# A dual attention kernel with a token gate: gate logits gathered in one bank with one transpose, the gate's load moved, and a new order of the whole

## The chip, the cores and the metric

The kernel runs on one core of one Trainium2 chip, in one launch. The metric is the device time in microseconds; the median of three runs stands for the kernel.

## The reference

One input x of 2048 tokens by 512 features passes through two branches, and a gate mixes them token by token. All arrays are bf16.

```python
g = sigmoid((x * gate_w).sum(-1, keepdims=True))
# A: softmax attention, H = 32 heads of Dh = 16
scores = einsum("bhqd,bhkd->bhqk", q, k) * Dh ** -0.5
a = einsum("bhqk,bhkd->bhqd", softmax(scores), v) ... @ A_wo
# B: linear attention with a learned feature map
phi(y) = concat([softmax(y @ w_phi), softmax(-y @ w_phi)])
kv = einsum("bhsf,bhsd->bhfd", phi(k), v);  z = phi(k) summed over s
b = (phi(q) @ kv) / (phi(q) @ z + 1e-6) ... @ B_wo
return g * a + (1 - g) * b
```

q, k and v of each branch come from x @ A_wqkv and x @ B_wqkv. Branch A needs 32 x 2048 x 2048 exponentials, and these are nearly all of the work.

## The kernel before

**Units and packs.** The scores of branch A are cut into units of 128 keys by 512 queries for one head. Four heads make a pack (four units, stacked in the four row groups of TensorE), 16 packs (all 2048 keys) make a head group, and 32 such groups (8 for each of the four token quarters) make 512 packs and 2048 units. `_scores` (L981) computes scores into PSUM. `_exp` (L1031) runs the exponential on ScalarE over three and two units in turn, through a ring of five PSUM banks, into the tile ET. `_values` (L1101) multiplies ET with V and sums the pack into one bank for the head group; V carries a column of ones, so the softmax sum comes with it. `_norm` transposes this sum in 32x32 blocks on VectorE (L1161), divides and transposes back.

**Units on VectorE.** Some units skip ScalarE. `SHARES` lists how many for each of the 32 head groups. `_plan_vector` (L835) places them, always as the fourth unit of a pack, and collects them in batches of `NB` = 5; `FIRST` and `LAST` give the sizes of the first and last batches, `SOON` four single packs near the start that are handled in two early batches. `_vector_batch` (L866) computes the scores of each unit into a bank, turns them into fixed-point bits on VectorE (L887, one instruction a unit), and then a cubic approximation of the exponential for the whole batch (L911, L913, L914, L915, L897) into the tile vu.

**Branch B and projections.** VectorE also copies out the projections (L703, L759, L783), does branch B's feature maps (L1272 and L1300 to L1354) and the normalizations. `K0`, `SK`, `Q0`, `SQ` are due times of branch B's parts, counted in packs.

**The order.** Every operation is registered with an engine, an assumed cost, a priority `prio` and a release `rel` (in packs). `Plan.order` simulates the engines and writes out a fixed order for each engine's queue; the waits on semaphores follow from the data. So at run time each engine works through a fixed list, and TensorE and SP stop at the first instruction whose input is missing. Assumed DMA sizes (`size`, in MB) only tell the simulation when data will land. `rel` is not a wait on the chip: it only decides the place in the list. Three PSUM banks outside the ring are handed to jobs (accumulators, projections, gate, VectorE's units) in that order.

**Loads.** `_loads` (L497) registers all loads on SP but one. Those of WA (A_wqkv) come in two parts, the first 128 columns of each of q, k, v at the start and the other 384 columns later, with `rel` = `XREL`. WB is B_wqkv, WoA and WoB are the output weights, and gw is the gate vector, in 2-byte pieces to 128 partitions. Two token quarters of x are transposed by DMA (L604), and so are two parts of WB (L1231).

**The gate.** `_gate` (L788) spreads the gate vector over 128 columns on POOL (gwb, L791). For each token quarter four matmuls (L800) give the quarter's logits, the same in all 128 rows of a bank of its own. VectorE transposes that bank in 32x32 blocks into T1 (L805) and copies one column out into gz (L808). Then come sign, one exponential (L816), plus one, and a copy to four partition groups (L822).

Of the kernel before, what the change touches and what calls it, by code (L numbers as in the profile page):

```python
# [7 lines left out]
ALU = mybir.AluOpType  # L8
AX = mybir.AxisListType

P = 128
# [6 lines left out]
F32, BF16 = dt.float32, dt.bfloat16  # L18
# [349 lines left out]
class _Kernel:  # L368
# [2 lines left out]
    NSLOT = 25  # L371
    VCP = 8 * 17 + 16
    NQS = 6
    NB, NVU, LEAD = 5, 3, 11
    QDUE, VPRIO, VREL, TPRIO = 27.0, -9.0, 161.0, 3
    KEEP = 14
    XREL, KD, VD = 12, 11, 5
    BYDMA = (2, 3)
    KREL = 2
    EARLY = 23  # L380
    VREL0 = 3
    FIRST = (2, 2)
    LAST = (3, 2)
    OREL = 0

    def __init__(self, nc, A_x, A_wqkv, A_wo, B_wqkv, B_w_phi, B_wo, gate_w, out):
        self.nc = nc
# [27 lines left out]
    def _memory(self, ctx):  # L415
        nc, S, NT, NQC = self.nc, self.S, self.NT, self.NQC
# [80 lines left out]
    def _loads(self):  # L497
        NT = self.NT
        B = Buf
        self.b_xn = [[B(), B()] for _ in range(self.NQC)]  # L500
        self.b_WA = [[B(), B()] for _ in range(3)]
        self.b_WB = [B(), B(), B()]
        self.b_WoA, self.b_WoB, self.b_wphi, self.b_gw = B(), B(), B(), B()
        self.b_wphin, self.b_heads = B(), B()
        WA3 = self.A_wqkv.rearrange("(c p) j -> p c j", p=P)
        x4 = self.x2d.rearrange("(t p) d -> p t d", p=P)

        WB3 = self.B_wqkv.rearrange("(c p) j -> p c j", p=P)

        def load_x(j, t0, n, prio, rel=-99):  # L510
            writes = self.b_xn[j] if n == 4 else [self.b_xn[j][t0 % 4 // 2]]
            self.dma("SP", f"x{j}{t0 % 4 // 2}", lambda e: e.dma_start(self.xn[:, t0:t0 + n, :], x4[:, t0:t0 + n, :]),
                     writes=writes, prio=prio, cost=0.53, rel=rel, size=0.131 * n)

        def load_wa(s, part, eng, prio, rel=-99):
            lo, hi = (0, P) if part == 0 else (P, D)
            self.dma(eng, f"wa{s}{part}", lambda e: e.dma_start(
                self.WA[:, s, :, lo:hi], WA3[:, :, D * s + lo:D * s + hi]), writes=[self.b_WA[s][part]], prio=prio,
                cost=0.54, rel=rel, size=0.131 if part == 0 else 0.393)

        def load_wb(s, prio, rel=-99):
            self.dma("SP", f"wb{s}", lambda e: e.dma_start(self.WB[:, s], WB3[:, :, D * s:D * s + D]),
                     writes=[self.b_WB[s]], prio=prio, rel=rel, cost=0.53, size=0.524)
# [16 lines left out]
        self.dma("SP", "gw", lambda e: e.dma_start(self.gw[:], self.gate_w.rearrange("(c p) -> p c", p=P),  # L540
                                                   allow_slow_non_contiguous=True),
                 writes=[self.b_gw], prio=-4, cost=0.53, rel=6, size=0.016)
# [244 lines left out]

    def _gate(self):  # L788
        op, NQC = self.plan.op, self.NQC
        b_gwb, last = Buf(), []  # L790
        op("POOL", lambda e: e.tensor_copy(self.gwb[:], self.gw[:, :, None].to_broadcast([P, 4, P])), 1.0,  # L791
           reads=[self.b_gw], writes=[b_gwb], name="gwb", prio=15)
        z = self.gz[:]
        for qc in range(NQC):
            job = Job()

            m = None
            for c in range(4):
                def mm(e, c=c, qc=qc, job=job):
                    return e.matmul(self._bank(job), self.gwb[:, c, :], self.xT[:, 4 * qc:4 * qc + 4, c],  # L800
                                    start=(c == 0), stop=(c == 3))
                m = op("PE", mm, self.c_pe(512), reads=[self.b_xT[qc], b_gwb], deps=[m], name="gate", prio=18 + qc,
                       rel=12, acquire=None if c else job)
            k = qc % 2
            t = op("DVE", lambda e, k=k, job=job: e.transpose(  # L805
                self.T1[:, k].rearrange("p b d -> p (b d)"), self._bank(job)), 0.65, deps=[m], name="gate_t",
                prio=18 + qc, writes=[self.b_T1[k]], release=job)
            last.append(op("DVE", lambda e, qc=qc, k=k: e.tensor_copy(self.gz[:, qc], self.T1[:, k, :, 0]), 0.2,  # L808
                           reads=[self.b_T1[k]], name="gate_c", prio=18 + qc))
        flat = self.gh[:].rearrange("p r q b -> p (r q b)")  # L810
        col = z.rearrange("p q b -> p (q b)")
        for r, sign in ((0, -1.0), (1, 1.0)):
            last.append(op("DVE", lambda e, r=r, sign=sign: e.tensor_scalar(
                self.gh[:, r].rearrange("p q b -> p (q b)"), col, sign, None, op0=ALU.mult), 0.2,
                deps=list(last), name="gate_z", prio=22))
        a = op("ACT", lambda e: e.activation(flat, flat, ACT.Exp), 0.2, deps=last, name="gate_exp", prio=24)  # L816
        self.b_g, self.b_hB = Buf(), Buf()
# [1 line left out]
               name="gate_h", prio=24)  # L819
        parts = []  # L820
        for j in range(4):
# [13 lines left out]
    def _plan_vector(self):  # L835
# [746 lines left out]
```

## Time and profile before

| | |
|---|---|
| median of 3 runs | 840.32 us (840.21 to 841.15) |
| the profiled execution, its own time | 842.38 us |
| its span, first to last instruction | 838.9 us |
| busy: TensorE / VectorE / ScalarE / POOL | 803.5 / 809.9 / 826.7 / 8.1 us |
| granted TensorE clock | 1.000 |

The engines are written PE (TensorE), PEld (its weight loads), DVE (VectorE), ACT (ScalarE), POOL (GpSimd) and SP. Times in the profile are of one profiled execution, which lies 3.48 us over its span and 2.06 us over the median of the runs. A group's line gives busy time, the mean of one instruction in ns, the idle time of the engine just before, and what ended most of that idle time. In a timeline, the first two columns are the start and the length in us, and a bracket at the end holds the engine's wait just before it. Instructions of one engine overlap a little, so the distance from one start to the next is the better cost of one.

### The profile page before, as it was taken

The page shows a single profiled execution, that of the slowest core. Times are in us where ns is not written, and L with a number is a line of the kernel's source. Part 1 is how long each engine was busy: PE and PEld are TensorE (multiplying, and loading weights), DVE is VectorE, ACT ScalarE, POOL GpSimd, SP SyncE. Part 2 cuts the span into 40 slices and gives each one's busy share as a digit, 9 for nine tenths or more (in the row PEclk, how much of TensorE's full clock was granted, in tenths as well). Part 3 has the DMA queues.
Part 4 walks back from the last instruction along what each step waited for, and adds up shares of the span by engine and source line. Part 5 has one row for each costly group of instructions (what it writes and reads, how often), then busy time and mean ns, then how long its engine had stood idle before and what let it go on. Part 6 is the DMA issues. An engine that isn't in the chain of part 4 may idle for free.

```text
span 838.9 us, 19684 instructions
## 1 busy us (share of the span) xinstructions
PE 803.5 (96%) x8800; PEld 265.3 (32%) x8800; DVE 809.9 (97%) x1055; ACT 826.7 (99%) x733; POOL 8.1 (1%) x14
## 2 busy tenths in 40 slices
PE   9999999999999999999999999999999999999998
PEld 4334233233322322232223222332223332222344
DVE  5999999999999999999999989999999999999996
ACT  7999999999999999999999999999999999999997
POOL 3000000000000000000000000000000000000000
PEclk9999999999999999999999999999999999999999
DMA  9600000000000000030003000320002110000000
GB/s 227 183 1 3 5 2 7 1 2 8 2 7 2 8 1 8 2 65 19 1 15 81 14 8 2 57 52 1 8 2 52 33 32 2 2 7 2 2 2 27
DMA packets 49027, 20.01 MB, mean 24 GB/s; under 512 B 38704, under 2 KB 48944, under 8 KB 48944
## 3 DMA queue, kind: packets, MB, share of 16 engines
q1 hardware_dynamic: 48272, 18.58, 9.9%
q8 instruction: 68, 1.11, 0.6%
q10 hardware_dynamic: 672, 0.20, 0.1%
q14 instruction: 15, 0.12, 0.1%
HBM read 6.31 MB, written 2.10 MB: 10 GB/s over the span
## 4 chain that ended last, share of the span: by engine, by line
ACT 75%; DVE 16%; PE 4%; DMA 2%; SPq 2%; issue 0%
ACT ET L1039 75%; DVE vt L887 2%; DVE vu L897 2%; PE ps L988 2%; DVE vf L914 1%; DMA WA<-in_A_wqkv_dram 1%; PE ps L1117 1%; DVE vu L915 1%; DVE bq L1272 1%; DVE vf L911 1%; DMA WB<-in_B_wqkv_dram 1%; DVE vt L1315 1%; PE ps L1108 1%; SPq L604 1%; DVE bq L1309 1%; DVE V L783 1%
## 5 line engine op out<-in xcount | busy, mean ns | idle before, releaser
L1039 ACT ACTIVATE ET<-ps 128x1536 bf16<-128x1536 f32 x728 | 824.4, 1381 | 2.8 <-PE ps L988 2.3
L988 PE MATMUL ps<-qT,kT 32*128 32x512 bf16 (+2 forms) x2248 | 318.3, 364 | 26.8 <-ACT ET L1039 20.6
L1117 PE MATMUL ps<-kT,zero 128*32 128x512 bf16 (+1 forms) x3100 | 259.9, 383 | 0.0
L1108 PE MATMUL ps<-ET,V 128*32 128x512 bf16 (+2 forms) x1993 | 196.3, 364 | 0.7 <-DVE vt L887 0.4
L988 PEld LDWEIGHTS ps<-qT,kT 32*128 32x128 bf16 x2248 | 84.0, 91 | 305.0 <-ACT ET L1039 217.6
L887 DVE TENSOR_SCALAR vt<-ps 128x512 uint32<-128x512 f32 x224 | 145.1, 678 | 4.5 <-PE ps L988 4.0
L897 DVE SCALAR_TENSOR_TENSOR vu<-vt,vu 128x2560 int16<-128x2560 uint32 (+2 forms) x47 | 126.4, 2690 | 0.5
L1117 PEld LDWEIGHTS ps<-kT,zero 128*32 128x32 bf16 x3100 | 70.2, 94 | 109.0 <-issue 82.5
L1108 PE MATMUL ps<-vu,V 128*32 128x512 bf16 (+1 forms) x255 | 84.1, 360 | 0.0
L1108 PEld LDWEIGHTS ps<-ET,V 128*32 128x32 bf16 x1993 | 56.1, 95 | 58.4 <-issue 31.0
L915 DVE TENSOR_TENSOR vu<-vu,vf 128x2560 f16<-128x2560 f16 (+2 forms) x49 | 67.8, 1385 | 0.5
L914 DVE TENSOR_TENSOR vf<-vf 128x2560 f16<-128x2560 f16 (+2 forms) x49 | 67.8, 1385 | 0.2
L911 DVE TENSOR_SCALAR vf<-vt 128x2560 f16<-128x2560 uint8 (+2 forms) x47 | 66.7, 1418 | 0.0
L681 PE MATMUL ps<-WB,xT 128*128 128x512 bf16 x192 | 55.4, 383 | 1.1 <-DVE T L1161 1.0
L913 DVE TENSOR_SCALAR vu<-vf 128x2560 f16<-128x2560 f16 (+2 forms) x49 | 37.6, 767 | 0.2
L681 PE MATMUL ps<-xT,WA 128*128 128x512 bf16 (+1 forms) x124 | 35.3, 379 | 1.5 <-DMA WA<-in_A_wqkv_dram 1.3
L1108 PEld LDWEIGHTS ps<-vu,V 128*32 128x32 bf16 x255 | 22.4, 96 | 13.0 <-issue 8.4
L1161 DVE STREAM_TRANSPOSE T<-ps 128x512 f32<-128x512 f32 (+1 forms) x35 | 23.1, 660 | 2.1 <-PE ps L1108 2.0
L681 PEld LDWEIGHTS ps<-WB,xT 128*128 128x128 bf16 x192 | 14.2, 97 | 26.7 <-issue 14.4
L1272 DVE TENSOR_SCALAR bq<-ps 128x512 bf16<-128x512 f32 x32 | 21.3, 679 | 0.6 <-PE ps L681 0.5
L777 PE MATMUL ps<-WA,xT 128*128 128x128 bf16 x256 | 19.3, 220 | 0.0
L1315 DVE TENSOR_TENSOR vt<-vt,brec 128x4096 bf16<-128x4096 bf16 (+1 forms) x10 | 18.6, 1864 | 0.3
(100 smaller groups left out, 432.3 us busy)
## 6 DMA issues: line engine op xcount, KB each, us to landing
qT<-qraw SPq DMA_DIRECT2D x120, 16.0 KB, 1.8
xn<-in_A_x_dram SPq DMA_DIRECT2D x3, 512.0 KB, 6.8
WB<-in_B_wqkv_dram SPq DMA_DIRECT2D x3, 512.0 KB, 6.1
out_dram<-WB SPq DMA_DIRECT2D x12, 128.0 KB, 1.7
WA<-in_A_wqkv_dram SPq DMA_DIRECT2D x3, 384.0 KB, 8.7
xn<-in_A_x_dram SPq DMA_DIRECT2D x2, 256.0 KB, 3.8
WoA<-in_A_wo_dram SPq DMA_DIRECT2D x1, 512.0 KB, 8.3
WoB<-in_B_wo_dram SPq DMA_DIRECT2D x1, 512.0 KB, 9.0
```

The lines of the kernel that those rows point to most:

```text
L681: mm = op("PE", lambda e, c=c: e.matmul(self._bank(job)[:, 0:n], lhs(c), rhs(c), start=(c == 0), stop=(c == 3)), self.c_pe(n), reads=reads ...
L887: parts.append(op("DVE", lambda e, j=j, job=job: e.tensor_scalar(vt[:, j, :], self._bank(job), SCALE * LOG2E * 2.0 ** 24, 2.0 ** 31, op0=A ...
L897: o = op("DVE", lambda e: e.scalar_tensor_tensor(out=flat(vu).bitcast(I16), in0=flat(vt), scalar=2.0 ** -17, in1=flat(vu), op0=ALU.mult, o ...
L911: ("_frac", two, lambda e: e.tensor_scalar(vf, frac, 1 / 256, ROOT, op0=ALU.mult, op1=ALU.add), [b_vt], [b_vf]),
L913: lambda e: e.tensor_scalar(vu, vf, CUBE, SQUARE, op0=ALU.mult, op1=ALU.add), [b_vf], [b_vu]),
L914: ("_sq", two, lambda e: e.tensor_tensor(vf, vf, vf, ALU.mult), [b_vf], [b_vf]),
L915: ("_cube", two, lambda e: e.tensor_tensor(vu, vu, vf, ALU.mult), [b_vf, b_vu], [b_vu]),
L988: ins = e.matmul(out[u][:, cols], self.kT[32 * i:32 * i + 32, cp, kt * TOK:(kt + 1) * TOK], self.qT[32 * i:32 * i + 32, s, q], start=True, ...
L1039: o = plan.op("ACT", lambda e: e.activation(self.ET[:, a % NS:a % NS + n, :], self.ps[:, a % NR:a % NR + n, :], ACT.Exp, scale=SCALE), sel ...
L1108: ins = e.matmul(self._bank(ot)[32 * i:32 * i + 32, to], self.V[:, kt, g8 // 2, v0:v0 + 32], tile[:, cols], start=first and j == 0, stop=o ...
L1117: ins = e.matmul(self._bank(ot)[32 * i:32 * i + 32, lo:QCH], self.zero[:], self.kT[:, 0, lo:QCH], start=False, stop=False, tile_position=( ...
L1272: [lambda e, b, k=k: e.tensor_scalar(bq[:, k].rearrange("p (g s v) -> p g s v", g=8, s=2)[:, :, 0, :], b.rearrange("p (g v) -> p g v", g=8 ...
```

## The change

The gate's four quarters share one bank. The buffer gwb is 136 columns wide, is set to zero, and gets the gate vector in columns 6, 38, 70 and 102. Reading 128 columns from column 6 - 2 qc puts the vector at column 2 qc of each group of 32, so quarter qc's logits land in rows 2 qc of every 32 rows and zeros are added to the others. All sixteen matmuls add into one bank, one transpose brings the logits out, and the sign is applied straight from T1, so the copies into gz are gone. The first gate matmul now needs all four quarters of x. The gate vector's load gets a later place (`rel` 12, priority -0.3, behind WoA at -1 and WoB at -0.5) and a larger assumed size. The rest are constants of the order: `XREL` 12 to 6 for the later parts of WA, a larger assumed size for them, other releases, priorities and due times, and other SHARES. With `ENDS` = 11 in place of 9 and eight units in place of nine in the last head group, the last of them lies in pack 510 of 0 to 511; before, none lay in the last four packs.

```diff
-    NB, NVU, LEAD = 5, 3, 11
-    QDUE, VPRIO, VREL, TPRIO = 27.0, -9.0, 161.0, 3
+    NB, NVU, LEAD = 5, 3, 26
+    QDUE, VPRIO, VREL, TPRIO = 27.0, -12.0, 161.0, 4
-    XREL, KD, VD = 12, 11, 5
+    XREL, KD, VD = 6, 11, 4
-    KREL = 2
-    EARLY = 23
-    VREL0 = 3
+    KREL = 3
+    EARLY = 19
+    VREL0 = 5
-    LAST = (3, 2)
-    OREL = 0
+    LAST = (4,)
+    OREL = 2
+    ENDS = 11
...
-        self.gwb = sb("gwb", [P, 4, P], BF16)
+        self.gwb = sb("gwb", [P, 4, P + 8], BF16)
-        self.gz = sb("gz", [P, NQC, 16], F32)
...
-                cost=0.54, rel=rel, size=0.131 if part == 0 else 0.393)
+                cost=0.54, rel=rel, size=0.131 if part == 0 else 0.45)
...
-                 writes=[self.b_gw], prio=-4, cost=0.53, rel=6, size=0.016)
+                 writes=[self.b_gw], prio=-0.3, cost=0.53, rel=12, size=0.1)
...
+        op("POOL", lambda e: e.memset(self.gwb[:], 0.0), 0.6, writes=[b_gwb], name="gwb_zero", prio=-10)
+        op("POOL", lambda e: e.tensor_copy(
+            self.gwb[:, :, 6:134].rearrange("p c (j r) -> p c j r", r=32)[:, :, :, 0],
+            self.gw[:, :, None].to_broadcast([P, 4, 4])), 0.3, reads=[self.b_gw, b_gwb], writes=[b_gwb], name="gwb", prio=15)
+        job, m = Job(), None
         for qc in range(NQC):
             for c in range(4):
+                def mm(e, c=c, qc=qc):
+                    return e.matmul(self._bank(job), self.gwb[:, c, 6 - 2 * qc:6 - 2 * qc + P],
+                                    self.xT[:, 4 * qc:4 * qc + 4, c], start=(qc + c == 0), stop=(qc + c == 6))
...
+        t = op("DVE", lambda e: e.transpose(self.T1[:, 0].rearrange("p b d -> p (b d)"), self._bank(job)), 0.65, deps=[m],
+               name="gate_t", prio=21, writes=[self.b_T1[0]], release=job)
+        z = self.T1[:, 0, :, 0:8].rearrange("p b (q h) -> p q b h", h=2)[:, :, :, 0]
...
-    SHARES = (0, 2, 1, 8, 1, 8, 3, 4, 10, 3, 7, 6, 10, 4, 12, 3,
-              2, 11, 10, 5, 13, 4, 7, 6, 14, 11, 4, 14, 6, 12, 14, 9)
+    SHARES = (0, 2, 1, 9, 2, 6, 3, 3, 9, 5, 8, 7, 12, 5, 8, 4,
+              2, 11, 12, 3, 12, 3, 10, 4, 15, 10, 5, 14, 4, 14, 15, 8)
...
-            at = (2 * k + 1) * 9 // (2 * n)
+            at = (2 * k + 1) * self.ENDS // (2 * n)
...
-    K0, SK, Q0, SQ = 17.0, 9.25, 178.0, 14.75
+    K0, SK, Q0, SQ = 17.0, 9.5, 176.5, 14.25
-    SOON = (8, 17, 18, 21)
-    SDUE = 37
+    SOON = (8, 18, 20, 21)
+    SDUE = 43
```

More of the change, by code (lines that the diff above doesn't have):

```diff
@@ L789, in _gate @@
         op, NQC = self.plan.op, self.NQC
[L790 to L793, printed above, removed]
+        b_gwb = Buf()
+        op("POOL", lambda e: e.memset(self.gwb[:], 0.0), 0.6, writes=[b_gwb], name="gwb_zero", prio=-10)
+        op("POOL", lambda e: e.tensor_copy(
+            self.gwb[:, :, 6:134].rearrange("p c (j r) -> p c j r", r=32)[:, :, :, 0],
+            self.gw[:, :, None].to_broadcast([P, 4, 4])), 0.3, reads=[self.b_gw, b_gwb], writes=[b_gwb], name="gwb", prio=15)
@@ L794, in _gate @@
+        job, m = Job(), None
         for qc in range(NQC):
-            job = Job()
-            m = None
             for c in range(4):
[L799 to L809, printed above, removed]
+                def mm(e, c=c, qc=qc):
+                    return e.matmul(self._bank(job), self.gwb[:, c, 6 - 2 * qc:6 - 2 * qc + P],
+                                    self.xT[:, 4 * qc:4 * qc + 4, c], start=(qc + c == 0), stop=(qc + c == 6))
@@ new lines, in _gate @@
+                m = op("PE", mm, self.c_pe(512), reads=[b_gwb] + (self.b_xT if m is None else []), deps=[m] if m else [], name="gate",
+                       prio=18 + qc, rel=12, acquire=None if m else job)
+        t = op("DVE", lambda e: e.transpose(self.T1[:, 0].rearrange("p b d -> p (b d)"), self._bank(job)), 0.65, deps=[m],
+               name="gate_t", prio=21, writes=[self.b_T1[0]], release=job)
+        z = self.T1[:, 0, :, 0:8].rearrange("p b (q h) -> p q b h", h=2)[:, :, :, 0]
+        last = []
@@ L810, in _gate @@
         flat = self.gh[:].rearrange("p r q b -> p (r q b)")
-        col = z.rearrange("p q b -> p (q b)")
         for r, sign in ((0, -1.0), (1, 1.0)):
             last.append(op("DVE", lambda e, r=r, sign=sign: e.tensor_scalar(
-                self.gh[:, r].rearrange("p q b -> p (q b)"), col, sign, None, op0=ALU.mult), 0.2,
+                self.gh[:, r], z, sign, None, op0=ALU.mult), 0.2, reads=[self.b_T1[0]],
                 deps=list(last), name="gate_z", prio=22))
```

## The prediction, on record before the run

> **What bounds the kernel now.** I read the page's first part, then the groups by line, ScalarE's timeline, the chain of waits in the first 32 us, and the windows. The groups first (busy us, mean ns, then idle time before them and its releaser):
>
> ```profile
> L1039 ACT ACTIVATE ET<-ps 128x1536 bf16<-128x1536 f32 x728 | 824.4, 1381 | 2.8 <-PE ps L988 2.3
> L887 DVE TENSOR_SCALAR vt<-ps 128x512 uint32<-128x512 f32 x224 | 145.1, 678 | 4.5 <-PE ps L988 4.0
> L805 DVE STREAM_TRANSPOSE T<-ps 128x512 f32<-128x512 f32 x4 | 2.9, 712 | 0.1
> L808 DVE COPY gz<-T 128x16 f32<-128x16 f32 x4 | 0.7, 164 | 0.0
> ```
>
> Exponentials fill 824.4 of the 838.9 us. ScalarE's timeline shows what the rest is:
>
> ```profile
> 7.33 1.45 ACT L1039 ACTIVATE ET<-ps 128x1536 bf16<-128x1536 f32 x1 [0.59 <-PE ps L988]
> 8.99 4.62 ACT L1039 ACTIVATE ET<-ps 128x1024 bf16<-128x1024 f32 x4 [0.21 <-PE ps L988]
> 13.80 15.93 ACT L1039 ACTIVATE ET<-ps 128x1024 bf16<-128x1024 f32 x14 [0.19 <-PE ps L988]
> 30.83 33.05 ACT L1039 ACTIVATE ET<-ps 128x1024 bf16<-128x1024 f32 x29 [1.10 <-PE ps L988]
> 63.74 0.33 ACT L816 ACTIVATE gh<-gh 128x128 f32<-128x128 f32 x1
> 63.94 111.06 ACT L1039 ACTIVATE ET<-ps 128x1536 bf16<-128x1536 f32 x98
> 175.25 658.73 ACT L1039 ACTIVATE ET<-ps 128x1536 bf16<-128x1536 f32 x582 [0.25 <-PE ps L988]
> ```
>
> So the time is a head of 7.33, then 826.65 us to 833.98 in which ScalarE loses about 2.2, then a tail of 4.9. Of the 2.2, one wait is 1.10. The chain of waits says whose it is:
>
> ```profile
> 18.33 0.66 SPq L522
> ...
> 19.04 0.53 SPq L540
> ...
> 19.61 0.51 SPq L522
> ...
> 20.16 0.51 SPq L517
> ...
> 20.71 8.67 DMA WA<-in_A_wqkv_dram
> ...
> 29.43 1.04 PE ps L681 x4
> 30.46 0.34 PE ps L988 x2
> ```
>
> SP issues branch B's weights (L522), the gate vector (L540), more B weights (L522) and only then the rest of WA (L517). The second WA load lands at 29.38. TensorE, in order, stands 1.34 us in front of its projection (from 28.09); the scores queued behind it release ScalarE late. VectorE is the second bound, in the windows (columns PE, PEld, DVE, ACT, POOL):
>
> ```profile
> 60.00:361.00 301.00, 290.46 (x2988) 94.06 (x2987) 297.94 (x420) 300.56 (x268) 0.00 (x0) 1.00 0.02 6
> 480.00:520.00 40.00, 37.22 (x401) 10.61 (x403) 36.71 (x44) 40.00 (x37) 0.00 (x0) 1.00 0.02 5
> ```
>
> VectorE idles 3.1 us in the 301, and 3.3 in the 40 around 500.
>
> **The change part by part.** ScalarE. SHARES sums to 224 before and 226 after; with the four of SOON, VectorE takes 230 units of the 2048 instead of 228, ScalarE 1818 instead of 1820. At 824.4/1820 = 0.453 us a unit that is -0.91 us, on the path. The gate's single exponential (0.33) stays.
>
> VectorE. Three of four transposes go: they stand 0.64 us apart from their successors (41.66 to 42.29), so 1.91. Four copies at about 0.11 (45.73 to 45.84) go: 0.44. Gate together -2.35. A batch of five units costs 5 x 0.60 (bits) + 1.40 + 0.73 + 1.40 + 1.40 + 2.73 = 10.66 by the chain's rows, 2.13 a unit, so two more cost +4.27. Batches stay 49 (47 and two early ones). Net +1.9 us on an engine with some 29 us idle, mostly at head and tail; 3.3 idle around 500 cover it. If that cover is gone, up to 1.9 us appears.
>
> TensorE. Sixteen gate matmuls stay sixteen of the same shape. They now hold one of the three free banks from first to last instead of four times a quarter; before, the four holdings spread from 40.1 to 57.7 us and TensorE waited 0.6 + 0.3 us on their transposes (L805). Bound: +0.9 if one long holding makes such waits anew, -0.9 if they go; ScalarE lost nothing between 30.83 and 63.7, so I take 0.
>
> SP's queue. XREL 12 to 6 with urgency -46 puts the three WA loads ahead of both B loads; the gate vector goes from between the B loads to behind both output weights (L544, L578). What the awaited load had in front after 18.33 was 512 + 1 + 512 + 384 KB, with itself 1793; now it has 384 + 384 = 768. The transposing DMA before it (issued 15.96, 4.4 to 5.0 to land) ends about 20.7. From there 1793 KB took 8.7 us, 206 KB/us, so 768 take 3.7: 24.4. At the worst end the whole old 8.67 from an issue at 18.9 gives 27.6. Both are before 28.09, so the 1.10 goes: bounds 0 (if the new order asks for WA correspondingly sooner) and -1.10. I take -1.10: size 0.45 for 0.393 also makes the order expect WA later. What is late next: B weights, about 768 KB/206 = 3.7 us later than before for the one read at 18.33, whose first matmul (L681 on WB) was at 35.27; it landed within 4.4 to 6.7 us of 18.33 (L522's rows), so some 6 us of cover remain. The other B load's transposing DMA was issued at 36.37. The gate vector: issue some 25.7 (behind L578's end), 5.2 us as in its row, 31 to 35; its matmuls began at 40.1. The output weights are first read at 429 us (L1448).
>
> POOL. One zero memset of 128x544 comes, by kvbd's row of that shape 0.64 us; the spread (0.81) shrinks. POOL idles 2.88 us up to 9.84, which hides it, if it does not hold VectorE: the two xT copies at 4.69 ran under the qT memset (4.52 to 6.33) and took 0.76; the two at 6.77, mostly without POOL work beside them, took 0.76 also. So 0; if it does hold a head copy there, up to +0.64. [...]
>
> Head otherwise: VREL0, KREL, VD, EARLY and SOON rearrange what TensorE does before 30 us. Waits of 0.21 and 0.19 stand there; bounds -0.4 and +0.6 (the largest other head wait, 0.59). I take 0.
>
> Tail: the last batch has four units instead of three and two, and one unit now lies in the last four packs. Its four-unit arithmetic lies between the two-unit row (0.69 + 0.42 + 0.65 + 0.69 + 1.22 = 3.7) and the five-unit one (7.7). The last such batch ended 829.58 and VectorE then stood 1.14 us idle. OREL = 2 moves output matmuls by two packs; they ran under the last normalization (834.50 to 835.83). Bounds -0.3 (the 0.30 TensorE stood idle at 835.89) and +1.1; I take 0, nearest to the covering rows. Due times of branch B and LEAD cost nothing themselves; what they do to VectorE's lateness is the third rival.
>
> **Sum.** 838.9 - 0.91 - 1.10 = 836.9 us span. The profiled execution took 842.38, span plus 3.48; the median is 840.32, 2.06 below that. I take the 2.01 off the median: 838.3. A difference of 0.2% is 1.7 us here, about what a measurement of this kernel can tell; its border is 838.6.
>
> **Rivals.** First, the wait only moves: TensorE's order asks for a B load, the gate vector or WA at another point just before it lands. For it: orders are fixed beforehand and transfers were late once already. Against: 3.7 us of cover for WA, 6 and more for the rest. It gives back the 1.10: 839.4.
>
> Second, the small waits go as well: 0.21, 0.19, 0.25 and some 0.5 of smaller ones, 1.1 in all: 837.2. For: the order is new everywhere. Against: they sit where projections and accumulations compete for banks, which stays.
>
> Third, slower: VectorE falls behind near 360 us. Cumulated SHARES ask for +5 units by the end of group 13 (16 packs of 1.613 us each, 14 groups, 7.33: 368 us): +10.65 - 2.35 = +8.3 us of work, where the window to 361 had 3.1 idle. That leaves it 5.2 us late. If values come that much later, TensorE waits at the end of a head group, the scores behind it wait too, and ScalarE stands up to 5.2 us: 838.3 + 5.2 = 843.5. It decides once the lateness passes what a head group can absorb. For: first uses follow the batch closely (L897 ends 352.2, used 352.97; ends 370.5, used 371.06), and the chain of waits runs through VectorE from 302 to 359. Against: a late unit need only be in before its group closes, and after the 1.10 and the two head waits only some 0.7 of ScalarE's 2.2 us can have gone to such bursts, though VectorE was 99% busy; VectorE even ran out of work around 500.
>
> Fourth, POOL's added memset holds a VectorE copy in the head for its 0.64 us, and the first scores come that much later: 838.9. For: it lies among the copies in front of 7.33. Against: the equal 0.76.
>
> **How the numbers follow.** Forecast 0.57 (own range 837.5 to 839.4; 0.5 of it below the border), first rival 0.17, second 0.05, third 0.17, fourth 0.04. Faster 0.5 + 0.05 = 0.55. Same 0.07 + 0.17 + 0.04 = 0.28. Slower 0.17. The range runs from the second rival, 837.2, into the third at 842.8, leaving out some 0.03 below and 0.12 above.
>
> **What would show it.** L1039 x727, near 823.5; no wait of about 1 us near 30 us; L517's three loads ahead of the second L522; L805 once, L808's copies gone, L887 at x226; ScalarE ending near 832. The forecast is wrong if ScalarE's waits after 60 us pass 2 us (third rival), if a wait of a transfer stands in TensorE's first 45 us (first), or if from the last exponential to the end it is over 5.5.

## The result: faster by 0.27%, with one term of the forecast missing and others in its place

The changed kernel takes 838.64 us (median of 11 runs, 838.39 to 839.23); the kernel before took 840.82 us in the same series (11 runs). The ratio is 0.9973, with a 95% interval of 0.9964 to 0.9982. The forecast was 838.3. The profiled execution of the changed kernel took 839.23 us with a span of 837.4; the other spans were 837.4 and 837.3, and eight from 836.6 to 837.0. Where executions of one kernel differ below, they mostly differ in the mean granted clock of TensorE, which is then given.

In the changed kernel, lines behind it are four lower (L1039 is L1035, L887 is L883, L805 is L803). The groups by line, in the columns used before:

```profile
L1035 ACT ACTIVATE ET<-ps 128x1536 bf16<-128x1536 f32 x728 | 823.8, 1379 | 1.1 <-PE ps L984 0.7
L883 DVE TENSOR_SCALAR vt<-ps 128x512 uint32<-128x512 f32 x226 | 147.1, 680 | 1.6 <-PE ps L984 1.1
L803 DVE STREAM_TRANSPOSE T<-ps 128x512 f32<-128x512 f32 x1 | 0.7, 710 | 0.0
```

One transpose is left of four, and the copies into gz have no line. VectorE computes 226 units here instead of 224, but ScalarE still has 728 exponentials. ScalarE's timeline:

```profile
7.95 41.08 ACT L1035 ACTIVATE ET<-ps 128x1536 bf16<-128x1536 f32 x36 [0.50 <-PE ps L984]
49.19 1.45 ACT L1035 ACTIVATE ET<-ps 128x1536 bf16<-128x1536 f32 x1 [0.17 <-PE ps L984]
50.54 0.30 ACT L812 ACTIVATE gh<-gh 128x128 f32<-128x128 f32 x1
50.74 781.79 ACT L1035 ACTIVATE ET<-ps 128x1024 bf16<-128x1024 f32 x691
834.76 0.38 ACT L1529 ACTIVATE xT<-ps 128x256 bf16<-128x256 f32 x1 [2.22 <-PE ps L1516]
```

The exponentials run from 7.95 to 832.53, 824.58 us instead of 826.65, so 2.07 less. Some 1.6 of this are waits: the one of 1.10 near 30 us is gone, and of the other 1.1 about 0.6 are left. The other 0.5 lie in the exponentials' own busy time, though they are as many and of the same two shapes as before. It goes with the waits too: over the profiles with 728 exponentials it grows with the number of pieces into which the timeline breaks. Their lengths add up to 824.1 to 824.3 us at three or four pieces (the changed kernel, e4_wa_late, e6_each_once), 824.6 to 825.3 at five to seven (824.8 at the six before) and 827.2 at twenty (e3_old_gate). Behind each wait the overlap with the instruction before is missing: alone, the two shapes took 1.45 and 1.02 us, in a row 2.37 together (e3_old_gate, 476.31). That is 0.10 us a piece; the sums give some 0.17 as an estimate, 2.9 us over 17 pieces. The tail, 4.87 us, is as it was. The head is 0.62 longer. Nearly all of this is TensorE's first projection, here before and then after, each from TensorE's timeline:

```profile
5.26 1.05 PE L715 MATMUL ps<-xT,WA 128*128 128x128 bf16 x16 [0.39 <-DVE xT L664]
```

```profile
5.38 1.65 PE L715 MATMUL ps<-xT,WA 128*128 128x128 bf16 x16 [0.18 <-DVE xT L664]
```

The same sixteen matmuls took 1.65 us instead of 1.05. Six experiments that keep the changed kernel's head show exponentials starting between 6.89 and 7.49, so this differs between executions of one order. It is also about the distance between the two groups of spans above: with a head as before, the profiled span would be 836.8, which is what most runs show.

SP's timeline shows the new order of loads: the three of WA, then the two of WB, and the gate vector last of all weights.

```profile
12.76 5.21 SPq L604 DMA_TRANSPOSE xT<-xn  x2
18.02 1.71 SPq L517 DMA_DIRECT2D WA<-in_A_wqkv_dram  x3
19.77 1.05 SPq L522 DMA_DIRECT2D WB<-in_B_wqkv_dram  x2
...
23.04 1.68 SPq L540 DMA_DIRECT2D gw<-in_gate_w_dram  x1
```

WA's loads now land in 4.2 us (median) instead of 8.7, and TensorE has no wait for a transfer between 5 and 45 us. The windows (PE, PEld, DVE, ACT, POOL, granted clock) show VectorE fuller around 500 us, 39.52 of 40 us instead of 36.71, while ScalarE loses nothing there:

```profile
60.00:361.00 301.00, 286.98 (x2983) 93.96 (x3006) 298.79 (x415) 300.68 (x266) 0.00 (x0) 1.00 0.04 8
480.00:520.00 40.00, 37.67 (x381) 11.49 (x373) 39.52 (x51) 40.00 (x36) 0.00 (x0) 1.00 0.03 8
```

### The profile page after: what moved, and what is told of

Read it like the earlier page. It is cut to its first block, busy times and chain, and to the rows that moved or that the text cites. A ratio compares the mean times of both kernels' runs of the same rounds, so it can differ in the third digit from the quotient of the medians.

```text
span 837.4 us, 19503 instructions
## 1 busy us (share of the span) xinstructions
PE 797.5 (95%) x8690; PEld 266.3 (32%) x8734; DVE 809.6 (97%) x1050; ACT 826.2 (99%) x733; POOL 8.0 (1%) x15
## 3 DMA queue, kind: packets, MB, share of 16 engines
HBM read 6.31 MB, written 2.10 MB: 10 GB/s over the span
## 4 chain that ended last, share of the span: by engine, by line
ACT 65%; DVE 30%; PE 4%; issue 0%
ACT ET L1035 65%; DVE vt L883 3%; DVE vu L893 3%; DVE vf L910 2%; DVE vu L911 2%; DVE vf L907 2%; PE ps L984 1%; DVE VB L1252 1%; DVE bq L1268 1%; DVE vt L1311 1%; DVE bq L1344 1%; DVE bq L1305 1%; DVE V L783 1%; DVE kT L703 1%; DVE vu L909 1%; DVE brec L1341 1%
## 5 line engine op out<-in xcount | busy, mean ns | idle before, releaser
L1035 ACT ACTIVATE ET<-ps 128x1536 bf16<-128x1536 f32 x728 | 823.8, 1379 | 1.1 <-PE ps L984 0.7
L984 PE MATMUL ps<-qT,kT 32*128 32x512 bf16 (+2 forms) x2250 | 324.0, 364 | 29.0 <-ACT ET L1035 19.8
L1113 PE MATMUL ps<-kT,zero 128*32 128x512 bf16 x3032 | 254.0, 383 | 0.0
L984 PEld LDWEIGHTS ps<-qT,kT 32*128 32x128 bf16 x2250 | 85.0, 91 | 306.3 <-ACT ET L1035 214.8
L883 DVE TENSOR_SCALAR vt<-ps 128x512 uint32<-128x512 f32 x226 | 147.1, 680 | 1.6 <-PE ps L984 1.1
L893 DVE SCALAR_TENSOR_TENSOR vu<-vt,vu 128x2560 int16<-128x2560 uint32 (+3 forms) x47 | 127.6, 2715 | 0.4
L1113 PEld LDWEIGHTS ps<-kT,zero 128*32 128x32 bf16 x3032 | 68.1, 95 | 105.7 <-issue 79.9
L911 DVE TENSOR_TENSOR vu<-vu,vf 128x2560 f16<-128x2560 f16 (+3 forms) x49 | 68.5, 1397 | 0.5
L910 DVE TENSOR_TENSOR vf<-vf 128x2560 f16<-128x2560 f16 (+3 forms) x49 | 68.6, 1399 | 0.3
L907 DVE TENSOR_SCALAR vf<-vt 128x2560 f16<-128x2560 uint8 (+3 forms) x47 | 67.0, 1425 | 0.1
L681 PE MATMUL ps<-WB,xT 128*128 128x512 bf16 x164 | 48.0, 382 | 3.1 <-issue 2.4
L909 DVE TENSOR_SCALAR vu<-vf 128x2560 f16<-128x2560 f16 (+3 forms) x49 | 37.9, 773 | 0.3 <-PE ps L1104 0.3
L681 PE MATMUL ps<-xT,WA 128*128 128x512 bf16 (+1 forms) x124 | 36.3, 380 | 0.7 <-DVE vt L883 0.6
L681 PEld LDWEIGHTS ps<-WB,xT 128*128 128x128 bf16 x192 | 13.9, 97 | 25.2 <-issue 14.6
```

What stands on the lines that cost most here:

```text
L681: mm = op("PE", lambda e, c=c: e.matmul(self._bank(job)[:, 0:n], lhs(c), rhs(c), start=(c == 0), stop=(c == 3)), self.c_pe(n), reads=reads ...
L883: parts.append(op("DVE", lambda e, j=j, job=job: e.tensor_scalar(vt[:, j, :], self._bank(job), SCALE * LOG2E * 2.0 ** 24, 2.0 ** 31, op0=A ...
L893: o = op("DVE", lambda e: e.scalar_tensor_tensor(out=flat(vu).bitcast(I16), in0=flat(vt), scalar=2.0 ** -17, in1=flat(vu), op0=ALU.mult, o ...
L907: ("_frac", two, lambda e: e.tensor_scalar(vf, frac, 1 / 256, ROOT, op0=ALU.mult, op1=ALU.add), [b_vt], [b_vf]),
L909: lambda e: e.tensor_scalar(vu, vf, CUBE, SQUARE, op0=ALU.mult, op1=ALU.add), [b_vf], [b_vu]),
L910: ("_sq", two, lambda e: e.tensor_tensor(vf, vf, vf, ALU.mult), [b_vf], [b_vf]),
```

## The experiments

### e1_wa_first and e5_gw_last: the order of loads alone

Both start from the kernel before and change nothing but SP's list. The first puts WA's three late loads ahead of both WB loads:

```diff
+            sp = queue["SP"]
+            late = [o for o in sp if o.name in ("dma_wa11", "dma_wa01", "dma_wa21")]
+            at = [o.name for o in sp].index("dma_wb2")
+            sp[:] = sp[:at] + late + [o for o in sp[at:] if o not in late]
```

> The kernel before, with one edit: in SP's list the three later WA loads stand ahead of both B loads and the gate vector. The lists of the four other engines are unchanged. Theory (the landing of WA is the 1.10 us): the wait of TensorE in front of the projection near 28 us and ScalarE's 1.10 at 30 us are gone, about -1.1 us, and nothing else moves. Rival (the order waits for the next late transfer instead): a wait of about 1 us on another load, time unchanged.

Measured: 839.99 us, ratio 0.9988 (0.9979 to 0.9997). Its ScalarE timeline has no wait of 1 us near 30 us:

```profile
9.01 4.62 ACT L1044 ACTIVATE ET<-ps 128x1024 bf16<-128x1024 f32 x4 [0.22 <-PE ps L993]
13.82 28.31 ACT L1044 ACTIVATE ET<-ps 128x1024 bf16<-128x1024 f32 x25 [0.19 <-PE ps L993]
42.41 20.63 ACT L1044 ACTIVATE ET<-ps 128x1536 bf16<-128x1536 f32 x18 [0.28 <-PE ps L993]
```

The second moves only the gate vector's load behind the output weights:

```diff
-                 writes=[self.b_gw], prio=-4, cost=0.53, rel=6, size=0.016)
+                 writes=[self.b_gw], prio=-0.3, cost=0.53, rel=12, size=0.1)
```

> The kernel before with one load moved: the gate vector goes to the end of SP's loads, behind both output weights. The other four engines' lists are unchanged, and WA stays behind both B loads. Theory (the 2-byte pieces of the gate vector hold up the loads behind them, since with the gate vector last and WA late there was no wait): WA lands in time, the wait near 30 us goes, about -1 us like the run with WA first. Rival (only WA's place counts): the wait stays, 0.

Measured: 840.42 us, ratio 0.9998 (0.9989 to 1.0006). The median span is 838.0, against 838.7 of the kernel before in that series and 837.9 in e1_wa_first. In its profile the wait is gone too, with WA still behind both WB loads, and WA lands in 6.7 us instead of 8.7. The first move is worth 0.8 us of span, close to the term of the sum; the second 0.7 of span, while its device time, 0.5 lower in the median, is not clear of the scatter. So either move seems enough. In e5_gw_last the chain of waits then runs through a transposed part of WB, 6.04 us up to its landing at 41.23, a next late transfer as in the rival of e1_wa_first, but ScalarE's waits near 42 us are only 0.17 us there and 0.28 in e1_wa_first. That the gate vector's 512 pieces of 2 bytes are what held WA back is possible, but not shown: e2_gate_only below has the gate vector at its old place, and its WA also landed in 6.7 us in the execution that was profiled, where the loads were issued 0.7 us earlier (from 17.64 instead of 18.33).

### e4_wa_late: the changed kernel with WA behind WB again

```diff
-    XREL, KD, VD = 6, 11, 4
+    XREL, KD, VD = 12, 11, 4
...
-                cost=0.54, rel=rel, size=0.131 if part == 0 else 0.45)
+                cost=0.54, rel=rel, size=0.131 if part == 0 else 0.393)
```

> The changed kernel with the WA loads back behind both B loads, by the old release and assumed size; only SP's list differs from the changed kernel. The gate vector stays last. Theory: the projection, reached near 28.25 us, waits again for a landing near 29, and ScalarE loses 0.5 to 1.1 us. Rival (the gate vector's 2-byte pieces made the landing late, not the B loads): no wait, 0.

Measured: 838.8 us, ratio 0.9974 (0.9965 to 0.9984), with exponentials over 824.58 us, as in the changed kernel. WA landed in 6.2 us. With the gate vector last, moving WA ahead adds nothing to the time.

### e2_gate_only: the gate alone, in the kernel before

The kernel before with the gate's part of the change (gwb of 136 columns, one bank, one transpose); loads and constants stay as they were, and the order follows.

```diff
-            job = Job()
...
+        job, m = Job(), None
...
+        t = op("DVE", lambda e: e.transpose(self.T1[:, 0].rearrange("p b d -> p (b d)"), self._bank(job)), 0.65, deps=[m],
+               name="gate_t", prio=21, writes=[self.b_T1[0]], release=job)
```

> The kernel before, with the gate alone changed: one bank, one transpose, no copies; the loads, SHARES and all constants of the order as before. VectorE does 2.35 us less. Theory of the prediction (that time is off the path): 0 within 0.3 us, and the 1.10 us wait near 30 us stays. Rival (small waits of ScalarE come from VectorE being full): the some 0.7 us of them after 60 us shrink, -0.5 us or so; a third case is a worse tail from the new order, up to +1.

Measured: 841.55 us, ratio 1.0006 (0.9998 to 1.0015). Its executions come in steps: 840.55 to 840.84 at a mean granted clock of 1.000, 841.5 to 841.7 at 0.998, 842.9 to 843.1 at 0.995. At full clock this equals the kernel before. The profiled execution, at 0.998, had waits of 0.33 and 0.65 at 362 to 364 us that the kernel before does not have. The end of its ScalarE timeline:

```profile
364.24 469.18 ACT L1034 ACTIVATE ET<-ps 128x1024 bf16<-128x1024 f32 x415 [0.65 <-PE ps L983]
837.21 0.38 ACT L1528 ACTIVATE xT<-ps 128x256 bf16<-128x256 f32 x1 [3.79 <-PE ps L1515]
```

Without those two waits the exponentials take 1.6 us less than before (1.10 of it is the wait near 30 us, which this execution does not have). But from the last exponential to the end it is 6.5 us instead of 4.9: the list that follows from the new gate puts seventeen output matmuls ahead of the last matmuls with V, and ScalarE's last copy waits 3.79 us instead of 2.22. That is the third case, a worse tail. So what the 2.35 us of VectorE are worth by themselves in the old order stays open; a gain and a loss cancel here. The steps led to the clock.

### e3_old_gate: the new order with the old gate

The reverse of e2_gate_only: the changed kernel, its loads and all its constants, with four banks, four transposes and four copies for the gate.

```diff
-        job, m = Job(), None
...
+            job = Job()
...
+            t = op("DVE", lambda e, k=k, job=job: e.transpose(
+                self.T1[:, k].rearrange("p b d -> p (b d)"), self._bank(job)), 0.65, deps=[m], name="gate_t",
+                prio=18 + qc, writes=[self.b_T1[k]], release=job)
```

> The changed kernel with the old gate: four banks, four transposes, four copies, every constant of the new order kept. VectorE gets 2.35 us more. Theory (ScalarE bounds, VectorE has cover): within 0.5 us of the changed kernel. Rival (VectorE is just as full and its end comes later): +2.4 us or more, seen as ScalarE waits after 60 us or as a tail over 5.5 us.

Measured: 853.55 us, ratio 1.0153 (1.0129 to 1.0176). The waits of ScalarE, and the window from 440 to 450 us:

```profile
ACT ET L1040 <- PE ps L989: 10.2, 18, 1.0
ACT xT L1534 <- PE ps L1521: 7.4, 1, 7.4
```

```profile
440.00:450.00 10.00, 9.67 (x44) 2.01 (x41) 7.85 (x9) 6.39 (x5) 0.00 (x0) 0.50 0.60 120
```

No theory had this size. In these 10 us TensorE is 97% busy but has a granted clock of 0.50 and finishes 44 matmuls, and ScalarE works 6.39 us. From the last exponential to the end it is 10.1 us instead of 4.9, the other sign that the rival named. The constants have no fixed worth: the list that they give with one gate is good, and with the other it is the worst one measured here.

### e6_each_once and e7_moved: the two units that ScalarE did not lose

SHARES of 15 in head groups 24 and 30 ask for 15 units where only 14 packs can give one: the places are lo + (2k+1) * 14 // 30, and two of the 15 coincide. So two units are in the batches twice. VectorE computes 226, but only 224 different ones leave ScalarE. The first kernel names each unit once:

```diff
-    LAST = (4,)
+    LAST = (3,)
...
-              2, 11, 12, 3, 12, 3, 10, 4, 15, 10, 5, 14, 4, 14, 15, 8)
+              2, 11, 12, 3, 12, 3, 10, 4, 14, 10, 5, 14, 4, 14, 14, 8)
```

> The changed kernel, with the two units that SHARES of 15 places twice computed once on VectorE (14 instead of 15 in two groups, and a last batch of three so that the other batches stay). ScalarE keeps its 1820 units, VectorE does 4.3 us less. Theory (ScalarE bounds this order): within 0.3 us of the changed kernel's 838.6. Rival (VectorE is on the path): 1 to 4 us faster.

Measured: 840.48 us, ratio 0.9993 (0.9984 to 1.0002). At a clock of 1.000 it ran in 838.24 to 838.72, as the changed kernel did; at 0.998 in about 840.4, at 0.996 in 841.3 to 841.7. So some 4 us of VectorE's work less (two units at the 2.13 us worked out in the prediction), late in the kernel, bring nothing, and the new order holds less well at full clock. The second kernel moves the two units to head group 18, so that ScalarE really has 1818:

```diff
-              2, 11, 12, 3, 12, 3, 10, 4, 15, 10, 5, 14, 4, 14, 15, 8)
+              2, 11, 14, 3, 12, 3, 10, 4, 14, 10, 5, 14, 4, 14, 14, 8)
```

> The changed kernel, with the two doubled units replaced by two other ones (14 instead of 12 in head group 18), so that VectorE has the same work as in the changed kernel and ScalarE really has 1818 units in 727 instructions. Theory (0.453 us a unit on the path): 0.9 us faster than the changed kernel, some 837.7. Rival (VectorE has no room in that group): ScalarE waits after 480 us take it back, 838.6 or more.

Measured: 841.01 us, ratio 1.0001 (0.999 to 1.0012); no run was at full clock (0.990 to 0.998), and the best, at 0.998, took 839.15. Its windows of 2 us, and ScalarE's timeline:

```profile
536.00:538.00 2.00, 1.02 (x7) 0.28 (x5) 2.00 (x3) 2.00 (x3) 0.00 (x0) 1.00 0.00 0
538.00:540.00 2.00, 1.65 (x9) 0.46 (x8) 2.00 (x4) 2.00 (x3) 0.00 (x0) 1.00 0.94 177
540.00:542.00 2.00, 1.86 (x15) 0.66 (x19) 2.00 (x6) 2.00 (x3) 0.00 (x0) 0.57 1.15 209
542.00:544.00 2.00, 2.00 (x27) 0.49 (x16) 1.75 (x4) 0.62 (x2) 0.00 (x0) 0.58 0.82 154
```

```profile
543.89 175.54 ACT L1035 ACTIVATE ET<-ps 128x1536 bf16<-128x1536 f32 x155 [1.38 <-PE ps L984]
720.14 48.65 ACT L1035 ACTIVATE ET<-ps 128x1024 bf16<-128x1024 f32 x43 [0.70 <-PE ps L984]
```

TensorE has little to do from 536 to 540 (2.67 of 4 us), then its clock falls to about half, the scores come late, and ScalarE stands 1.38 us. In the changed kernel the same 4 us hold 3.74 us of work, and the clock stays at 1.00. This was a coincidence in time until the filling matmuls were taken away (e9_no_fill).

### e8_reordered: 1817 units, other constants

The cut below shows the new SHARES and due times of branch B; VPRIO, TPRIO, EARLY, LAST, ENDS and SDUE differ too.

```diff
-    SHARES = (0, 2, 1, 9, 2, 6, 3, 3, 9, 5, 8, 7, 12, 5, 8, 4,
-              2, 11, 12, 3, 12, 3, 10, 4, 15, 10, 5, 14, 4, 14, 15, 8)
+    SHARES = (0, 2, 3, 8, 2, 5, 4, 4, 9, 6, 6, 9, 11, 7, 6, 3,
+              3, 13, 11, 2, 13, 5, 7, 6, 13, 8, 6, 14, 4, 14, 14, 9)
...
-    K0, SK, Q0, SQ = 17.0, 9.5, 176.5, 14.25
+    K0, SK, Q0, SQ = 16.5, 9.5, 178.5, 13.25
```

> The changed kernel with other constants: SHARES of 227 units, none above 14 in a group (ScalarE has 1817), LAST = (3, 2), ENDS = 9, other due times of branch B and other priorities. Theory (units times 0.453 us, and small waits of ScalarE set by the order): 1.4 us off for three units and up to 0.5 for small waits, 836.7 to 837.3. Rival (a full VectorE, or gaps on TensorE that pull its granted clock down as with the old gate in the new order): 839 or more, with a clock under 1.000.

Measured: 838.33 us, ratio 0.997 (0.9959 to 0.9981). One run at full clock took 837.02 (span 835.0); those at 0.998 took 837.8 to 838.8, those at 0.996 839.3 to 839.5. Its profile, at 0.996, has two falls, at 363 to 367 and 787 to 791 us, with ScalarE waits of 0.70 and 1.02 behind them. In the one run where the clock held, three units less come with 1.6 us less, for 1.4 worked out; the other constants moved too.

### e9_no_fill: is it the order that lowers the clock?

`_fill` puts matmuls whose weights are zero (L1113) into TensorE's list. They change no value. This kernel leaves them out where the order places them between 500 and 508 us, so that 7 are left of 52 there in the profiles; all other lists and TensorE's other instructions stay.

```diff
+            queue = p.order()["PE"]
+            lo, hi = 500.0, 508.0
+            queue[:] = [o for o in queue if o.name != "pad" or not lo <= o.start < hi]
+            for o in queue:
+                if lo <= o.start < hi:
+                    o.filled = 0
```

> The changed kernel with its zero-weight filling matmuls (L1113) left out where the order places them between about 500 and 508 us; nothing else moves. The stretch was at full granted clock in the changed kernel, with TensorE busy 1.76 to 1.86 of each 2 us. Theory (a few thin microseconds lower the granted clock, and that makes the scores late): granted clock about 0.5 for some 4 us between 502 and 512, scores late there, ScalarE waits of 1 to 2 us there that the changed kernel doesn't have, and 839.6 to 840.6 us. Rival (the dips of the earlier runs come from the chip and not from the order): clock 1.00 there as before, 838.6, or less where a filling matmul was in the way.

Measured: 841.73 us (11 runs, 841.4 to 842.43), ratio 1.0011 (1.0002 to 1.002); 3.1 us more than the changed kernel, with a clock of 0.992 to 0.994 in every run. The window of 3.4 us in the changed kernel, then windows and ScalarE's timeline of this one:

```profile
500.00:503.40 3.40, 3.16 (x47) 1.01 (x39) 3.37 (x3) 3.40 (x4) 0.00 (x0) 1.00 0.02 5
```

```profile
500.00:503.40 3.40, 2.34 (x26) 0.69 (x22) 3.40 (x2) 3.40 (x4) 0.00 (x0) 1.00 0.02 5
503.40:506.80 3.40, 3.09 (x21) 0.57 (x19) 3.33 (x7) 3.40 (x4) 0.00 (x0) 0.53 0.00 0
513.60:517.00 3.40, 3.40 (x14) 0.83 (x13) 1.29 (x2) 1.63 (x2) 0.00 (x0) 0.50 0.00 0
517.00:520.40 3.40, 3.32 (x34) 0.95 (x32) 2.51 (x4) 2.91 (x4) 0.00 (x0) 0.96 0.14 46
```

```profile
509.24 5.13 ACT L1040 ACTIVATE ET<-ps 128x1536 bf16<-128x1536 f32 x4 [0.48 <-PE ps L989]
516.14 1.45 ACT L1040 ACTIVATE ET<-ps 128x1536 bf16<-128x1536 f32 x1 [1.77 <-PE ps L989]
518.08 317.54 ACT L1040 ACTIVATE ET<-ps 128x1024 bf16<-128x1024 f32 x281 [0.49 <-PE ps L989]
```

Less work on TensorE made the kernel slower. With 2.34 instead of 3.16 us of TensorE work in 3.4, the clock went to 0.50 at about 503.6 and stayed there until 517.3, though TensorE was busy nearly all that time. All eleven runs show the lower clock, and only the fillers differ, so here it is the order that lowers the clock, by a thin stretch. The fall was over three times as long as expected, and the cost about twice.

### e10_gate_time and e12_gate_behind: the gate's time on VectorE put back

In both, every engine's list is the changed kernel's, and three more transposes of 128x512 are added to gate instructions. In the first they read the gate's bank, before it is released:

```diff
+        def four(e):
+            for k in range(2):
+                e.transpose(self.onTA[:, 2, 2 * k:2 * k + 2].rearrange("p a b -> p (a b)").bitcast(F32), self._bank(job))
+            e.transpose(self.T1[:, 1].rearrange("p b d -> p (b d)"), self._bank(job))
+            return e.transpose(self.T1[:, 0].rearrange("p b d -> p (b d)"), self._bank(job))
```

> The changed kernel with VectorE's freed gate time put back: the one transpose of the gate's bank is done four times, into four places, so 3 x 0.71 = 2.1 us more of VectorE at about 45 us; every engine's list is otherwise the changed kernel's. Theory (VectorE's time there lies off the path): the same within 0.3 us, 838.3 to 839.0, with VectorE later by 2.1 us only until its next idle stretch. Rival (the restructured gate's freed time on VectorE is where the gain came from): 840.7, with waits of ScalarE on late values at 60 to 360 us.

Measured: 845.09 us, ratio 1.0037 (1.0023 to 1.005): 842.3 in two runs at a clock of 0.998, 845.1 in four at 0.994. From TensorE's waits (for whom, in total, times, the longest): the one that the gate's transpose ends in the changed kernel, and then the same one here:

```profile
PE ps L1236 <- DVE T L803: 0.3, 1, 0.3
```

```profile
PE ps L1240 <- DVE T L807: 2.1, 1, 2.1
```

```profile
46.00:48.00 2.00, 0.38 (x7) 0.00 (x0) 2.00 (x4) 1.65 (x2) 0.00 (x0) 1.00 0.00 0
48.00:50.00 2.00, 1.52 (x19) 0.66 (x19) 2.00 (x6) 0.78 (x1) 0.00 (x0) 1.00 0.00 0
50.00:52.00 2.00, 2.00 (x17) 0.42 (x16) 1.86 (x5) 1.50 (x2) 0.00 (x0) 0.52 0.00 0
```

TensorE asks for the gate's bank at once. It stands 2.1 us, its clock falls to 0.5 from 50 to 60 us, and ScalarE loses 5.5 us in all, all of it before 61 us. My theory fell, and the rival had the sign, but a third to a half of the size and another place for the waits. The second kernel asks whether it was only the held bank: here the transposes read the copy in SBUF, behind the release.

```diff
+            spots = ((2, 0),) if r == 0 else ((2, 2), (1, 0))
+            def more(e, r=r, sign=sign, spots=spots):
+                for i, k in spots:
+                    e.transpose(self.onTA[:, i, k:k + 2].rearrange("p a b -> p (a b)").bitcast(F32),
+                                self.T1[:, 0].rearrange("p b d -> p (b d)"))
+                return e.tensor_scalar(self.gh[:, r], z, sign, None, op0=ALU.mult)
```

> The changed kernel with three more transposes on VectorE again, as in e10_gate_time, but behind the gate's bank instead of in front of its release: they turn the already freed copy in SBUF (one ahead of the first L809, two ahead of the second), some 2.0 us at 47 to 51 us. Every list is the changed kernel's. Theory (e10's loss was TensorE standing 2.1 us for the gate's bank, with the clock's fall behind it; VectorE's time by itself is nearly free): no idle stretch of TensorE over 1 us near 46 to 52 us, clock 1.00, 838.3 to 839.3. Rival (VectorE's evictions of 47 to 52 us free banks that TensorE asks for at once, so that the time counts wherever it lies): TensorE idle some 0.7 us near 48 and 1.3 near 51, a fall of the clock behind it, and 840.5 to 845.

Measured: 842.02 us (11 runs), ratio 1.0013 (1.0004 to 1.0022): 841.1 and 841.25 at full clock, about 842 at 0.998, 843.1 to 843.5 at 0.996. TensorE's waits from 44 to 60 us:

```profile
PE ps L1243 <- DVE vt L890: 1.6, 1, 1.6
...
PE ps L1243 <- DVE T L803: 0.3, 1, 0.3
```

The gate's bank comes free as early as in the changed kernel, but the next bank, freed by the bits of a unit (L890), comes 1.57 us late. The rival was right in the main, with one gap instead of two: in this stretch VectorE's evictions free the banks that TensorE asks for, and 2 us of VectorE cost 2.5 to 2.6 us even at full clock.

### e11_no_thin: a version that beats both

The changed kernel with constants chosen so that the order has no stretch that is thin in full matmuls, and with each unit named once (227 and the four of SOON, 1817 on ScalarE):

```diff
-    NB, NVU, LEAD = 5, 3, 26
-    QDUE, VPRIO, VREL, TPRIO = 27.0, -12.0, 161.0, 4
-    KEEP = 14
+    NB, NVU, LEAD = 5, 3, 29
+    QDUE, VPRIO, VREL, TPRIO = 27.0, -23.0, 161.0, -5
+    KEEP = 13
...
-    EARLY = 19
+    EARLY = -58
...
-    LAST = (4,)
+    LAST = (4, 2)
...
-    ENDS = 11
+    ENDS = 9
...
-    SHARES = (0, 2, 1, 9, 2, 6, 3, 3, 9, 5, 8, 7, 12, 5, 8, 4,
-              2, 11, 12, 3, 12, 3, 10, 4, 15, 10, 5, 14, 4, 14, 15, 8)
+    SHARES = (0, 2, 2, 7, 2, 6, 4, 5, 8, 8, 2, 5, 14, 9, 11, 2,
+              1, 9, 11, 5, 13, 6, 12, 2, 9, 14, 6, 12, 10, 10, 11, 9)
...
-    K0, SK, Q0, SQ = 17.0, 9.5, 176.5, 14.25
+    K0, SK, Q0, SQ = 16.5, 9.5, 182.0, 14.5
...
-    SDUE = 43
+    SDUE = 64
```

> The changed kernel with other constants of the order: 227 different units and the four early ones on VectorE, no unit named twice, 1817 on ScalarE (the changed kernel: 1820), and an order chosen so that no few microseconds of it are thin in full matmuls. Theory (units count on ScalarE at 0.453 us each, and the clock stays full where no stretch is thin): clock 1.000 in all runs, three units less are -1.4 us, so 837.2 (836.6 to 837.8). Rival (the clock's dips are not foreseen by the order's thin stretches): clock 0.996 to 0.999 in some runs as in the earlier reordered kernel, 838.3. Second rival (units moved to VectorE come back as late values): full clock and 838.6 or more.

Measured: 836.7 us (5 runs, 836.24 to 837.12), ratio 0.9949 (0.9937 to 0.996); the clock was 1.000 in four runs and 0.999 in the fastest. ScalarE's timeline, and the group of exponentials:

```profile
7.88 44.73 ACT L1035 ACTIVATE ET<-ps 128x1536 bf16<-128x1536 f32 x39 [0.50 <-PE ps L984]
52.44 0.35 ACT L812 ACTIVATE gh<-gh 128x128 f32<-128x128 f32 x1
52.64 777.76 ACT L1035 ACTIVATE ET<-ps 128x1024 bf16<-128x1024 f32 x688
```

```profile
L1035 ACT ACTIVATE ET<-ps 128x1536 bf16<-128x1536 f32 x727 | 822.2, 1386 | 0.8 <-PE ps L984 0.5
```

From 7.88 to 830.40 the exponentials have no single wait that the timeline breaks at. Here the group is x727, and 1.6 us of busy time are gone for three units less. Since the changed kernel keeps its full clock too, this run bears out the price of a unit rather than the cause of the falls.

## Why the prediction was right, and where only its number was

**ScalarE's two units, -0.91: wrong.** The step that failed is "ScalarE 1818 instead of 1820". I summed SHARES and did not follow the places that `_plan_vector` derives from it; two of the 226 coincide. ScalarE kept 1820 units (x728). The price of a unit was sound: three fewer took 1.6 us in e11_no_thin, for 1.4 worked out.

**The wait for WA, -1.10: right in size, too narrow in its cause.** WA landed 4.2 us after its issue near 18 us, in time by several us. But I counted the gate vector as 1 KB among 1793. By the spans of e5_gw_last and the times of e4_wa_late its move alone does about as much as WA's. The profiled execution of e2_gate_only, with its loads in the old order, had no such wait either, so the kernel before may not have it in every execution: over the runs this term is worth some 0.8 (e1_wa_first).

**Other small waits, taken as 0: about -1.0.** The second rival, -1.1 for these, came true in large part: 0.5 of waits are gone, and 0.5 of lost overlap with them. Which of the constants removed them no run isolates. They filled the place of the failed -0.91. Two errors of opposite sign met, so 838.3 for 838.64 is no proof of the sum. The base was off as well: I took 840.32, the median of three runs; eleven give 840.82, and from there the same sum is 838.8.

**VectorE, 0: right in the sum, wrong in its reason.** I set -2.35 us at 45 us against +4.27 us later, as if VectorE's time were one account, covered by 3.3 idle us around 500. The extra work did go there (39.52 of 40 us busy). But e12_gate_behind shows that 2 us at 47 to 51 us cost 2.5 to 2.6 in this order, and e6_each_once shows that some 4 us late in the kernel cost nothing at full clock. So VectorE's time at the gate is on the path of the new order; for the old order e2_gate_only leaves it open. The price "up to 1.9" for a cover that is gone was too low: in e10_gate_time 2.1 us on a held bank, with the fall of the clock behind it, cost 3.7 to 6.5 us.

**TensorE's bank, 0 within 0.9: right.** One wait of 0.3 us stands on the gate's transpose instead of 0.6 and 0.3. **POOL, 0: right.** The memset ran from 6.32 to 6.95 and the two copies at 7.29 took 0.76 us, so the fourth rival did not occur. Here no copy ran beside this memset. The two copies that ran from 4.81 beside the memset of qT (4.51 to 6.31) took 415 to 425 ns each, like the two at 7.29. **Head, 0 within -0.4 to +0.6:** +0.62 in the profile, nearly all of it the first projection, whose time differs between executions. **Tail, 0: right,** 4.87 against 4.92.

**The first rival** did not occur: TensorE waits for no transfer in 5 to 45 us; the gate vector was there at 30.7, its matmuls began at 38.2. **The third,** VectorE late near 360 us, did not occur either: ScalarE has no wait after 60 us that its timeline breaks at.

**What no case of mine held** is the clock. Every rival dealt with a late input or a held engine. The slower orders here lost much of their time behind falls of the granted clock (means of 0.984 to 0.992 in e3_old_gate, 0.992 to 0.994 in e9_no_fill, 0.994 to 0.998 in e10_gate_time); the changed kernel shows 1.000 in all eleven runs; what in the kernel before makes its times wider at the same clock is open. My slower case, +5.2 us by late values, did not occur; orders near this one did lose 3 to 15 us, in large part behind these falls, which I did not have.

## What to carry to other kernels

Where the order is fixed beforehand, a constant is worth only what the resulting list is worth: judge the list, and count what it does (units, places, loads), not what the constants say. VectorE's microseconds are not interchangeable: 2 us at 47 to 51 us cost 2.5 to 2.6 in e12_gate_behind, some 4 us late in the kernel nothing in e6_each_once, both at full clock. Price them by who asks for the bank that they free, at that moment. And a filler on TensorE may be worth its place: 45 fewer cost 3.1 us in e9_no_fill. Before removing work from an engine off the path, look at the granted clock.

## What the hardware showed that I had not expected

The granted clock fell although TensorE hardly stood still. In e9_no_fill the longest gap ahead of the fall was 0.63 us, and TensorE was busy for 2.34 of 3.4 us. How long a fall lasted follows from the clock in windows of 2 us. In e8_reordered it was 0.91, 0.50 and 0.74 from 362 to 368 us, and 0.72, 0.50 and 0.92 from 786 to 792: both times 3.4 us at half rate. In e12_gate_behind it was 0.86, 0.50 and 0.78 from 52 to 58 us, 3.4 again; e10_gate_time gives 10.2 and e9_no_fill 13.6: one, three and four times 3.4. The mean clocks fit: 3.4 us at half rate are 0.002 of 838 us, so 0.998 is one such fall, 0.994 three and 0.992 four (e7_moved and e2_gate_only also show values between). Runs of one kernel that differ by 0.002 in the mean clock differ by 0.6 (e9_no_fill) to 1.9 us (e6_each_once) of time.

No stretch of 3.4 us ahead of these falls was idle: the longest gap seen was 2.1 us, in e10_gate_time. Why one list falls in some executions and not in others (means of 1.000 to 0.996 in e6_each_once and in e12_gate_behind) no run shows, and how much work keeps the clock stays open. The 4 us from 536 held 2.67 busy us in e7_moved, but in e8_reordered the 4 us from 360 held 3.49 and those from 784 held 3.41, the last 0.4 and 1.1 us of them already at half rate, while the changed kernel kept its clock with 3.24 of 4 (595 to 599 us). The profile's busy time counts a 32-row matmul (L984, 364 ns) nearly like a 128-row one (L681, 380 ns), so it may not be the measure.

It is also open why the clock stayed low for 13.6 us in e9_no_fill while TensorE shows 3.09 to 3.40 of each 3.4 us busy, and why the first projection took 1.05 us in the kernel before, 1.16 in e4_wa_late and 1.65 in the changed kernel, with a granted clock of 1.00 shown in the first and the last.
